# GQA decode step with a gated MLP: one w_out block in 16-row chunks over 4 row groups, the side table over 2, and half of wo folded

## The chip, the cores and the metric

The kernel runs on one core of one Trainium2 chip. The metric is the device time of one execution in microseconds (us); the figures below are the runs of the kernel before and one profiled execution of it. Engines are named as the profile names them: PE (TensorE matmuls), PEld (its weight loads), DVE (VectorE), ACT (ScalarE), POOL (GpSimd), SP (SyncE, which issues most of the loads). SPq and ACTq are the sequencers that issue DMAs. q1 is the DMA queue of SP's transfers, q10 that of ACT's; both are served by the same 16 DMA engines.

## The reference

One decode step with 8 batches, a width of 512, and everything in float32:

```python
xn = layernorm(x)                                   # x: (8, 1, 512)
q = (xn @ wq) -> (8, 32 heads, 1, 128)              # wq: (512, 4096)
k, v = caches (8, 8 kv heads, 4096, 128), each kv head for 4 query heads
p = softmax(q k^T / sqrt(128));  s = (p v) @ wo     # wo: (4096, 512)
z = gelu(xn @ w_in)                                 # w_in: (512, 1792)
z1 = z[:, :896];  z2 = layernorm(z[:, 896:])
g = w_sp * z2 + b_sp                                # w_sp, b_sp: one number each
gate = silu((z1 * g) @ w_out)                       # w_out: (896, 512)
out = x + s * gate
```

The two caches are 134 MB each, so nearly all of the 291 MB that the kernel reads is K and V.

## The kernel before

**Buffers.** Large loads go through a ring of three buffers of 128 partitions x 64 KB (`slot()`). They are used in this order: the MLP's weights (w_in and a part of w_out) in the first, `wq` in the second, the first half of K for head 0 in the third. The second half of K for head 0 takes the first buffer again, V's first half the second, and so on: for each of 8 heads two halves of K and two of V, 8 MB each, and at the end wo, also 8 MB, in seven pieces (`WO_PIECES`: 8, 8, 8, 4, 2, 1 and 1 of its 32 rows of heads). All of these are issued by SP in program order, and each waits until its buffer is free. Free means that every instruction that reads or writes the buffer has finished.

**Small loads.** ACT issues three: x (L52), the side table `side_sb` (L54), and `w_low` (L61). The side table has 128 rows of 130 numbers (520 bytes): x once more in the layout of the output, and in its last two columns w_sp and b_sp. `w_low` is the part of w_out that is not in the MLP's load: three of its seven blocks of 128 rows, cut into chunks of 32 rows. It lies in DRAM as 8 groups (`LOW_E`) of 4 rows, with 64 numbers of padding at the end of each group, and lands on 32 partitions of the first buffer. `from_slot` gives out what is left of the first buffer: to xn, to hT, and to e.

**The MLP** (`mlp()`) runs ahead of the projections. PE multiplies xn by w_in (L140), with four column groups of the array (32 columns each, output partitions 32 g to 32 g + 31) at work on four quarters of the columns. GELU and the layernorm of the second half follow on DVE, ACT and POOL. L171 applies w_sp and b_sp from the side table, L173 multiplies by z1. The product is transposed (L176 for the first 128 columns of each quarter into hT, L180 for the others in four chunks of 32 into hL), copied out of PSUM, and multiplied with w_out: L184 four blocks from the MLP's load, one in each column group; L188 the three blocks of w_low, four chunks for each. L190 to L200 bring the sum into the output's layout and form the gate.

**Behind it** PE runs `project_q` (L207, L213) for the two groups of four kv heads, then for each head the scores (L230), the softmax, and the values (L273, L282). `scr` is a pair of PSUM buffers which all short results take in turn.

**The end.** wo's rows of heads 0 to 27 (`FOLDED`) are multiplied at full width of 512 columns, with the four query heads of a kv head in the four column groups (L324). DVE copies this sum out (L327), and PE adds the four groups with the matrix `same` (L338). The last four rows of heads are multiplied in the output's layout directly, in four parts of 128 columns (L333), two ahead of the fold and two behind. DVE multiplies by the gate (L343), adds x from the side table (L344), and SP stores.

Of the kernel before, what the change touches and what calls it, by code (L numbers as in the profile page):

```python
# [13 lines left out]
P = 128  # L14
B, D = 8, 512
HKV, REP, S, DH = 8, 4, 4096, 128
NK = D // P
G = 4
J = S // (G * P)
R = 32  # L20
FH = 896
FQ = 256
NB = FH // P
# [3 lines left out]
UNIT = 2 * G * 512  # L27
SLOT = HALF * UNIT
WO_PIECES = [(0, 8), (8, 16), (16, 24), (24, 28), (28, 30), (30, 31), (31, 32)]
FOLDED = HKV * REP - REP  # L30
QR = P // 4
LOW_E = 8
N_LOW = (NB - G) * 4 * D


@with_exitstack
def tile_gqa_gmlp_decode(ctx: ExitStack, tc: tile.TileContext, x, side, kT, v, wq, wo,
                         w_mlp, w_low, out):
    nc = tc.nc
# [7 lines left out]
    def slot():  # L47
        return ring.tile([P, SLOT], F32, name="slot")
# [2 lines left out]
    x_sb = const.tile([B, D], F32, name="x_sb")  # L51
    nc.scalar.dma_start(x_sb, x)  # L52
    side_sb = const.tile([P, P + 2], F32, name="side_sb")
    nc.scalar.dma_start(side_sb, side)  # L54

    mlp_slot = slot()
    n_in, n_mlp = NK * 2 * FH, NK * 2 * FH + G * D
    n_low = n_mlp + N_LOW
    nc.sync.dma_start(mlp_slot[:, :n_mlp], w_mlp)
    w_in_sb = mlp_slot[:, :n_in].rearrange("p (k n) -> p k n", k=NK)  # L60
    nc.scalar.dma_start(mlp_slot[:QR, n_mlp:n_low],  # L61
                        w_low[:, :P // (4 * LOW_E) * N_LOW].rearrange("e (i n) -> e i n", n=N_LOW))
    w_out_sb = mlp_slot[:, n_in:n_mlp].rearrange("p (j d) -> p j d", j=G)
    w_low_sb = mlp_slot[:QR, n_mlp:n_low].rearrange("p (j a d) -> p j a d", a=4, d=D)
    spare = [n_low]

    def from_slot(rows, n):
        lo = spare[0]
        spare[0] = lo + n
        return mlp_slot[:rows, lo:lo + n]  # L70
# [6 lines left out]
    ident = const.tile([P, P], F32, name="ident")  # L77
# [26 lines left out]
    def scratch(shape, name):  # L104
        t = ps.tile([P, 512], F32, name="scr")
        n = 1
        for s in shape[1:]:
            n *= s
        return t[:shape[0], :n]
# [18 lines left out]
    def mlp():  # L128
        zu = work.tile([P, 4, FQ], F32, name="zu", tag="p")
        z, u = zu[:, :2], zu[:, 2:]  # L130
        hy = work.tile([P, 2 * D], F32, name="hy", tag="pT")
        y_sb, hL = hy[:, :D], hy[:QR, D:].rearrange("p (a s) -> p a s", a=4)
        pz = scratch([P, 2 * FQ], "pz")
        nc.vector.memset(pz, 0.0)
        for part in range(2):
            for k in range(NK):
                for g in range(G):
                    lo = g * FQ
                    n = min(FQ, FH - lo)
                    nc.tensor.matmul(pz[R * g:R * (g + 1), part * FQ:part * FQ + n], xnT[:, k, :],  # L140
                                     w_in_sb[:, k, part * FH + lo:part * FH + lo + n],
                                     start=(k == 0), stop=(k == NK - 1))
        zf, uf = z.rearrange("p a f -> p (a f)"), u.rearrange("p a f -> p (a f)")
        nc.vector.tensor_copy(zf, pz)
        nc.vector.tensor_mul(uf, zf, zf)
        nc.vector.tensor_scalar(uf, uf, 0.044715, 1.0, op0=ALU.mult, op1=ALU.add)
        nc.vector.tensor_mul(uf, uf, zf)
        nc.scalar.activation(uf, uf, AF.Tanh, scale=GELU_C)
        nc.vector.tensor_scalar(uf, uf, 1.0, 0.5, op0=ALU.add, op1=ALU.mult)
        nc.vector.tensor_mul(zf, uf, zf)  # L150

        def mean(src, name):
            part_sum = small.tile([P, 1], F32, name="part_sum")
            nc.vector.tensor_reduce(part_sum, src, op=ALU.add, axis=AX.X)
            pm = scratch([P, 1], "pm")
            nc.tensor.matmul(pm, same_all, part_sum, start=True, stop=True)
            t = small.tile([P, 1], F32, name=name)
            nc.vector.tensor_scalar(t, pm, 1.0 / FH, None, op0=ALU.mult)
            return t

        z1, z2 = z[:, 0, :], z[:, 1, :]
        mu = mean(z2, "mu")
        nc.vector.tensor_scalar(z2, z2, mu, None, op0=ALU.subtract)
        nc.vector.tensor_mul(u[:, 0, :], z2, z2)
        nc.vector.memset(u[(G - 1) * R:, 0, FH - (G - 1) * FQ:], 0.0)
        var = mean(u[:, 0, :], "var")
        nc.vector.tensor_scalar(var, var, EPS, None, op0=ALU.add)
        rs = small.tile([P, 1], F32, name="rs")
        nc.gpsimd.tensor_tensor(rs, var, neg_half, op=ALU.pow)
        nc.vector.tensor_scalar(z2, z2, rs, None, op0=ALU.mult)  # L170
        nc.vector.tensor_scalar(z2, z2, side_sb[:, P:P + 1], side_sb[:, P + 1:P + 2],  # L171
                                op0=ALU.mult, op1=ALU.add)
        nc.vector.tensor_mul(u[:, 1, :], z2, z1)  # L173
        hT = from_slot(P, P)
        th = scratch([P, P], "th")
        nc.tensor.transpose(th, u[:, 1, :P], ident)  # L176
        nc.vector.tensor_copy(hT, th)
        tl = scratch([QR, 4 * P], "tl")
        for a in range(4):
            nc.tensor.transpose(tl[:, a * P:(a + 1) * P], u[:, 1, P + a * QR:P + (a + 1) * QR], ident)  # L180
        nc.vector.tensor_copy(hL.rearrange("p a s -> p (a s)"), tl)
        pw = scratch([P, D], "pw")
        for g in range(G):
            nc.tensor.matmul(pw[R * g:R * (g + 1), :], hT[:, R * g:R * (g + 1)], w_out_sb[:, g, :],  # L184
                             start=True, stop=(g == G - 1))
        for a in range(4):
            for g in range(NB - G):
                nc.tensor.matmul(pw[R * g:R * (g + 1), :], hL[:, a, R * g:R * (g + 1)],  # L188
                                 w_low_sb[:, g, a, :], start=False, stop=(a == 3))
        nc.vector.tensor_copy(y_sb, pw)  # L190
        py = scratch([P, P], "py")
        for g in range(G):
            nc.tensor.matmul(py[R * g:R * (g + 1), :], same[:, 0, :], y_sb[:, g * P:(g + 1) * P],
                             start=True, stop=True)
        e = from_slot(P, P)
        nc.vector.tensor_scalar(e, py, -1.0, 87.0, op0=ALU.mult, op1=ALU.min)
        nc.scalar.activation(e, e, AF.Exp)
        nc.vector.tensor_scalar(e, e, 1.0, None, op0=ALU.add)
        nc.vector.reciprocal(e, e)
        nc.vector.tensor_mul(gate, py, e)  # L200
# [88 lines left out]
    def load_v(h, half, parts):  # L289
# [4 lines left out]
        return t.rearrange("p (i j e) -> p i j e", i=HALF, j=J)  # L294

    mlp()
    project_q(0)
    project_q(1)
# [22 lines left out]
    part, acc = sc[:, 0, :], sc[:, 1, :P]  # L321
    for m in range(FOLDED):
        h, r = divmod(m, REP)
        nc.tensor.matmul(part[R * r:R * r + B, :], oT[:, h, r, :], wo_sb[:, m, :],  # L324
                         start=(m < REP), stop=(m >= FOLDED - REP))
    part_sb = work.tile([P, D], F32, name="part_sb", tag="p")
    nc.vector.tensor_copy(part_sb, part)  # L327

    def last_head(lo, hi):
        for m in range(lo, hi):  # L330
            h, r = divmod(m, REP)
            for g in range(G):
                nc.tensor.matmul(acc[R * g:R * g + B, :], oT[:, h, r, :], wo_sb[:, m, g * P:(g + 1) * P],  # L333
                                 start=(m == FOLDED), stop=(m == HKV * REP - 1))

    last_head(FOLDED, FOLDED + 2)
    for g in range(G):
        nc.tensor.matmul(acc[R * g:R * g + B, :], same[:, 0, :B], part_sb[:, g * P:(g + 1) * P],  # L338
                         start=False, stop=False)
    last_head(FOLDED + 2, HKV * REP)  # L340

    res = const.tile([P, P], F32, name="res")
    nc.vector.tensor_mul(res, acc, gate)  # L343
# [42 lines left out]
```

## Time and profile before

| What | us |
|---|---|
| median of 3 runs | 685.25 (685.02 to 686.68) |
| the profiled execution | 687.51 |
| its span, first to last instruction | 685.7 |
| PE busy | 379.4 (55% of the span) |
| DVE busy | 173.8 (25%) |
| ACT busy | 13.5 (2%) |
| mean granted TensorE clock | 0.755 of full |

A time in the profile counts from the first instruction, so all positions in what follows are within the span of 685.7. The profiled execution itself is 1.8 us longer than its span and 2.3 us above the median.

How to read the lines: a line of a timeline begins with the start and the duration in us, then engine, source line, operation, and output<-inputs; `x24` is the number of instructions merged, and brackets hold the idle time ahead of it with what ended it. A float32 matmul is two instructions. In a list of waits the numbers are the total, the count and the longest. In a list of DMA queues they are packets, MB, and the time of those packets as a share of 16 engines over the stretch asked for; under it, a list of issues gives the size and the median time from the issue until the data is seen. A line of stretches gives its bounds, its length, the busy time of PE, PEld, DVE, ACT and POOL with the instructions, then the granted clock, the DMA share and GB/s.

### The profile page before, as it was taken

What the parts mean: (1) busy time and instruction counts of PE and PEld (TensorE: products, weight loads), DVE (VectorE), ACT (ScalarE), POOL (GpSimd) and SP (SyncE); (2) the same over time, 40 slices, a digit from 0 to 9 for tenths busy, and PEclk for the clock granted to TensorE, in tenths of its full rate; (3) what the DMA queues carried; (4) which work ended last, traced back from release to release, by engine and by line L of the source; (5) the groups of instructions that cost most, each with busy time, mean ns of one, the idle gap of its engine ahead of it and who ended that gap; (6) DMA issues with size and microseconds to landing.
All of it is one profiled execution on the core that took longest, in us unless ns stands there. A gap on an engine that the chain in (4) does not pass through costs nothing.

```text
span 685.7 us, 5701 instructions
## 1 busy us (share of the span) xinstructions
PE 379.4 (55%) x2557; PEld 113.3 (17%) x2557; DVE 173.8 (25%) x371; ACT 13.5 (2%) x27; POOL 3.7 (1%) x11
## 2 busy tenths in 40 slices
PE   1486464546665455455754464555655355555665
PEld 1121121112111111111211021111211021111221
DVE  2422042402430033401431024401421024401450
ACT  0000000000000000000000000000000000000000
POOL 1000000000000000000000000000000000000000
PEclk9768677767778777777787777767778777767787
DMA  9999999999999999999999999999999999999994
GB/s 402 421 448 422 428 429 432 444 432 440 425 429 432 433 440 440 429 433 428 429 432 429 424 440 433 443 433 432 433 432 426 428 429 440 441 432 438 399 427 182
DMA packets 6704, 291.23 MB, mean 425 GB/s; under 512 B 752, under 2 KB 1008, under 8 KB 1400
## 3 DMA queue, kind: packets, MB, share of 16 engines
q1 hardware_dynamic: 6480, 290.00, 98.1%
q10 hardware_dynamic: 200, 0.87, 0.3%
q8 instruction: 20, 0.33, 0.2%
q14 instruction: 4, 0.03, 0.0%
HBM read 290.80 MB, written 0.07 MB: 424 GB/s over the span
## 4 chain that ended last, share of the span: by engine, by line
DMA 81%; PE 17%; DVE 1%; issue 0%; ACTq 0%; SPq 0%
DMA slot<-in_kT 35%; DMA slot<-in_v 35%; PE sc L230 7%; PE o_ps L273 6%; DMA slot<-in_wo 6%; DMA slot<-in_w_low 5%; PE scr L207 1%; PE scr L188 1%; PE sc L324 1%; PE po_ps L282 0%; DVE o_sb L278 0%; DVE o_all L276 0%; PE sc L333 0%; SPq L310 0%; DVE q_sb L210 0%
## 5 line engine op out<-in xcount | busy, mean ns | idle before, releaser
L230 PE MATMUL sc<-slot,qz 128*32 128x512 f32 x1024 | 147.9, 742 | 135.9 <-DMA slot<-in_kT 135.9
L273 PE MATMUL o_ps<-slot,pT 128*16 128x512 f32 x1024 | 152.1, 734 | 75.0 <-DMA slot<-in_v 75.0
L276 DVE TENSOR_TENSOR o_all<-o_ps,diag 128x512 f32<-128x512 f32 x64 | 44.2, 691 | 149.6 <-PE o_ps L273 149.6
L235 DVE TENSOR_REDUCE nm<-sc 128x1 f32<-128x1024 f32 x8 | 9.8, 1224 | 280.5 <-PE sc L230 280.5
L230 PEld LDWEIGHTS sc<-slot,qz 128*32 128x32 f32 x1024 | 36.0, 133 | 241.4 <-DMA slot<-in_kT 140.1
L278 DVE TENSOR_REDUCE o_sb<-o_all 128x128 f32<-128x512 f32 x64 | 67.9, 1062 | 2.2
L273 PEld LDWEIGHTS o_ps<-slot,pT 128*16 128x16 f32 x1024 | 29.7, 111 | 155.4 <-issue 106.5
L282 PE MATMUL po_ps<-fold,o_sb 128*128 128x4 f32 x128 | 24.9, 264 | 28.0 <-DVE o_sb L278 28.0
L282 PEld LDWEIGHTS po_ps<-fold,o_sb 128*128 128x128 f32 x128 | 19.2, 189 | 72.9 <-DVE o_sb L278 72.9
L261 PE MATMUL scr<-ident,p 128*128 128x128 f32 x64 | 14.5, 404 | 10.7 <-DVE p L256 10.7
L237 ACT ACTIVATE p<-sc,nm 128x1024 f32<-128x1024 f32 x8 | 8.9, 1114 | 577.6 <-DVE nm L235 577.6
L263 DVE COPY pT<-scr 128x128 f32<-128x128 f32 x64 | 13.9, 283 | 9.2 <-PE scr L261 9.2
L261 PEld LDWEIGHTS scr<-ident,p 128*128 128x128 f32 x64 | 11.6, 207 | 11.1 <-issue 11.1
L324 PE MATMUL sc<-slot,oT 128*8 128x512 f32 x56 | 9.4, 800 | 3.2 <-DMA slot<-in_wo 3.2
L140 PE MATMUL scr<-slot,xnT 128*32 128x256 f32 (+1 forms) x64 | 5.6, 494 | 8.5 <-DMA slot<-in_w_mlp 8.5
L207 PE MATMUL scr<-slot,xnT 128*32 128x512 f32 x64 | 8.6, 686 | 0.0
L240 PE MATMUL scr<-ident,nm 128*1 128x128 f32 x8 | 2.2, 270 | 10.9 <-DVE nm L235 10.9
L188 PE MATMUL scr<-slot,hy 32*32 32x512 f32 x24 | 7.0, 1055 | 1.2 <-DMA slot<-in_w_low 1.2
L253 PE MATMUL scr<-wl,same 128*128 128x1 f32 x16 | 3.2, 271 | 6.2 <-DVE wl L251 6.2
L256 DVE TENSOR_SCALAR p<-p,w 128x1024 f32<-128x1024 f32 x8 | 6.0, 753 | 0.3
L219 DVE COPY qz<-scr 128x4 f32<-128x4 f32 x64 | 4.6, 148 | 1.5 <-PE scr L213 1.5
L140 PEld LDWEIGHTS scr<-slot,xnT 128*32 128x32 f32 x64 | 3.1, 148 | 10.6 <-issue 10.2
(86 smaller groups left out, 61.5 us busy)
## 6 DMA issues: line engine op xcount, KB each, us to landing
slot<-in_v SPq DMA_DIRECT2D x4, 2048.0 KB, 40.2
slot<-in_wo SPq DMA_DIRECT2D x3, 2048.0 KB, 41.6
slot<-in_w_mlp SPq DMA_DIRECT2D x1, 4608.0 KB, 13.7
slot<-in_wo SPq DMA_DIRECT2D x1, 1024.0 KB
slot<-in_w_low ACTq DMA_DIRECT2D x1, 768.0 KB
slot<-in_wo SPq DMA_DIRECT2D x1, 512.0 KB, 33.1
slot<-in_wo SPq DMA_DIRECT2D x2, 256.0 KB, 26.7
slot<-in_kT SPq DMA_DIRECT2D x16, 48.3
```

Source lines behind the costliest of these rows:

```text
L188: nc.tensor.matmul(pw[R * g:R * (g + 1), :], hL[:, a, R * g:R * (g + 1)], w_low_sb[:, g, a, :], start=False, stop=(a == 3))
L207: nc.tensor.matmul(pq[R * g:R * (g + 1), :], xnT[:, k, :], wq_sb[:, k, lo:lo + REP * DH], start=(k == 0), stop=(k == NK - 1))
L230: nc.tensor.matmul(sc[R * g:R * (g + 1), c, :], qz[:, h, b * R:(b + 1) * R], k_sb[:, i, c, g, :], start=(b == 0), stop=(b == B - 1))
L235: nc.vector.tensor_reduce(m, sc, op=ALU.max, axis=AX.XY, negate=True)
L237: nc.scalar.activation(p.rearrange("p j s -> p (j s)"), sc.rearrange("p c s -> p (c s)"), AF.Exp, bias=m, accum_out=l[:, h:h + 1])
L261: nc.tensor.transpose(t[:, j * P:(j + 1) * P], p[:, 4 * c + j, :], ident)
L263: nc.vector.tensor_copy(pT[:, 4 * c + j].rearrange("p b (g r) -> p g b r", g=G), t[:, j * P:(j + 1) * P].rearrange("p (g b r) -> p g b r", ...
L273: nc.tensor.matmul(of[R * c:R * c + G * REP, :], pT[:, j, b, :], v_unit[:, j], start=(j < G), stop=(j >= J - G))
L276: nc.vector.tensor_mul(o_all, o, diag[:, :, None].to_broadcast([P, G, DH]))
L278: nc.vector.tensor_reduce(o_sb, o_all.rearrange("p g d -> p d g"), op=ALU.add, axis=AX.X)
L282: nc.tensor.matmul(po[:, b * REP:(b + 1) * REP], o_sb, fold, start=True, stop=True)
L324: nc.tensor.matmul(part[R * r:R * r + B, :], oT[:, h, r, :], wo_sb[:, m, :], start=(m < REP), stop=(m >= FOLDED - REP))
```

## The change

Three things change.

- **w_out.** Six blocks (0, 2, 4, 6, 3, 5) come with the MLP's load, whose rows grow from 36,864 to 40,960 bytes. Block 1 alone is left in w_low, as 8 chunks (`CH`) of 16 rows, loaded as 4 groups of 4 rows on 16 partitions. hT now holds both halves of the transposed product, hL has 8 chunks, each copied by an instruction of its own. The main matmuls are 6 (block j in column group j // 2), the low ones 8, all of block 1, so in column group 0.
- **The side table** lies in DRAM as 2 padded groups of 64 rows and is loaded in that shape.
- **wo.** `FOLDED` is 16: rows of heads 0 to 15 are folded, 16 to 31 go direct, eight ahead of the fold and eight behind.

hT, y_sb and e move out of the first buffer's spare room into the work tiles hy and zu; hL moves into it.

```diff
-FOLDED = HKV * REP - REP
-QR = P // 4
-LOW_E = 8
-N_LOW = (NB - G) * 4 * D
+FOLDED = 16
+LOW_E, LOW_R = 4, 4
+QR = LOW_E * LOW_R
+CH = -(-P // QR)
+MAIN = [0, 2, 4, 6, 3, 5]
+LOW = [1]
+SIDE_E = 2
+SIDE_N = P // SIDE_E * (P + 2)
+N_LOW = len(LOW) * CH * D
...
-    nc.scalar.dma_start(side_sb, side)
+    nc.scalar.dma_start(side_sb, side[:, :SIDE_N].rearrange("e (p n) -> e p n", n=P + 2))
...
     nc.scalar.dma_start(mlp_slot[:QR, n_mlp:n_low],
-                        w_low[:, :P // (4 * LOW_E) * N_LOW].rearrange("e (i n) -> e i n", n=N_LOW))
+                        w_low[:, :LOW_R * N_LOW].rearrange("e (i n) -> e i n", n=N_LOW))
...
-        y_sb, hL = hy[:, :D], hy[:QR, D:].rearrange("p (a s) -> p a s", a=4)
+        hy2 = from_slot(P, CH * P).rearrange("p (a s) -> p a s", a=CH)
+        hT = hy[:, :2 * P].rearrange("p (a s) -> p a s", a=2)
+        hL = hy2[:QR]
+        y_sb, e = zu[:, :2].rearrange("p a f -> p (a f)"), zu[:, 2, :P]
...
-        hT = from_slot(P, P)
-        th = scratch([P, P], "th")
-        nc.tensor.transpose(th, u[:, 1, :P], ident)
-        nc.vector.tensor_copy(hT, th)
-        tl = scratch([QR, 4 * P], "tl")
-        for a in range(4):
-            nc.tensor.transpose(tl[:, a * P:(a + 1) * P], u[:, 1, P + a * QR:P + (a + 1) * QR], ident)
-        nc.vector.tensor_copy(hL.rearrange("p a s -> p (a s)"), tl)
+        th = scratch([P, 2 * P], "th")
+        for a in range(2):
+            nc.tensor.transpose(th[:, a * P:(a + 1) * P], u[:, 1, a * P:(a + 1) * P], ident)
+        nc.vector.tensor_copy(hT.rearrange("p a s -> p (a s)"), th)
+        for lo in range(0, CH, 4):
+            n = min(4, CH - lo)
+            tl = scratch([QR, n * P], "tl")
+            for a in range(lo, lo + n):
+                k = min(QR, P - a * QR)
+                nc.tensor.transpose(tl[:k, (a - lo) * P:(a - lo + 1) * P],
+                                    u[:, 1, P + a * QR:P + a * QR + k], ident)
+            for a in range(lo, lo + n):
+                k = min(QR, P - a * QR)
+                nc.vector.tensor_copy(hL[:k, a], tl[:k, (a - lo) * P:(a - lo + 1) * P])
         pw = scratch([P, D], "pw")
-        for g in range(G):
-            nc.tensor.matmul(pw[R * g:R * (g + 1), :], hT[:, R * g:R * (g + 1)], w_out_sb[:, g, :],
-                             start=True, stop=(g == G - 1))
-        for a in range(4):
-            for g in range(NB - G):
-                nc.tensor.matmul(pw[R * g:R * (g + 1), :], hL[:, a, R * g:R * (g + 1)],
-                                 w_low_sb[:, g, a, :], start=False, stop=(a == 3))
+        for i, j in enumerate(MAIN):
+            g, a = divmod(j, 2)
+            nc.tensor.matmul(pw[R * g:R * (g + 1), :], hT[:, a, R * g:R * (g + 1)], w_out_sb[:, i, :],
+                             start=(a == 0), stop=(j in (3, 5, 6)))
+        for a in range(CH):
+            k = min(QR, P - a * QR)
+            for i, j in enumerate(LOW):
+                g = j // 2
+                nc.tensor.matmul(pw[R * g:R * (g + 1), :], hL[:k, a, R * g:R * (g + 1)],
+                                 w_low_sb[:k, i, a, :], start=False, stop=(a == CH - 1))
...
-        e = from_slot(P, P)
...
-    last_head(FOLDED, FOLDED + 2)
+    late_wo(FOLDED, FOLDED + 8)
     for g in range(G):
         nc.tensor.matmul(acc[R * g:R * g + B, :], same[:, 0, :B], part_sb[:, g * P:(g + 1) * P],
                          start=False, stop=False)
-    last_head(FOLDED + 2, HKV * REP)
+    late_wo(FOLDED + 8, HKV * REP)
...
-        "side": side.reshape(P, P + 2),
+        "side": np.concatenate([side.reshape(SIDE_E, SIDE_N), np.zeros((SIDE_E, 64), np.float32)], axis=1),
```

`late_wo` is `last_head` under a new name, with the same body.

More of the change, by code (lines that the diff above doesn't have):

```diff
@@ L53, in tile_gqa_gmlp_decode @@
     side_sb = const.tile([P, P + 2], F32, name="side_sb")
-    nc.scalar.dma_start(side_sb, side)
+    nc.scalar.dma_start(side_sb, side[:, :SIDE_N].rearrange("e (p n) -> e p n", n=P + 2))
     mlp_slot = slot()
-    n_in, n_mlp = NK * 2 * FH, NK * 2 * FH + G * D
+    n_in, n_mlp = NK * 2 * FH, NK * 2 * FH + len(MAIN) * D
     n_low = n_mlp + N_LOW
@@ L61, in tile_gqa_gmlp_decode @@
     nc.scalar.dma_start(mlp_slot[:QR, n_mlp:n_low],
-                        w_low[:, :P // (4 * LOW_E) * N_LOW].rearrange("e (i n) -> e i n", n=N_LOW))
-    w_out_sb = mlp_slot[:, n_in:n_mlp].rearrange("p (j d) -> p j d", j=G)
-    w_low_sb = mlp_slot[:QR, n_mlp:n_low].rearrange("p (j a d) -> p j a d", a=4, d=D)
+                        w_low[:, :LOW_R * N_LOW].rearrange("e (i n) -> e i n", n=N_LOW))
+    w_out_sb = mlp_slot[:, n_in:n_mlp].rearrange("p (j d) -> p j d", d=D)
+    w_low_sb = mlp_slot[:QR, n_mlp:n_low].rearrange("p (j a d) -> p j a d", a=CH, d=D)
     spare = [n_low]
@@ L327, in tile_gqa_gmlp_decode, with late_wo @@
     nc.vector.tensor_copy(part_sb, part)
-    def last_head(lo, hi):
+    def late_wo(lo, hi):
         for m in range(lo, hi):
@@ L361 @@
     w2 = c(B_w_out).reshape(NB, P, D)
-    rows = P // (4 * LOW_E)
-    low = np.zeros((LOW_E, rows * N_LOW + 64), np.float32)
-    low[:, :rows * N_LOW] = w2[1::2].reshape(NB - G, 4, LOW_E, rows, D).transpose(2, 3, 0, 1, 4).reshape(LOW_E, -1)
+    low = np.zeros((len(LOW), CH * QR, D), np.float32)
+    low[:, :P] = w2[LOW]
+    low = low.reshape(len(LOW), CH, LOW_E, LOW_R, D).transpose(2, 3, 0, 1, 4).reshape(LOW_E, -1)
+    low = np.concatenate([low, np.zeros((LOW_E, 64), np.float32)], axis=1)
     arrays = {
         "x": x,
-        "side": side.reshape(P, P + 2),
+        "side": np.concatenate([side.reshape(SIDE_E, SIDE_N), np.zeros((SIDE_E, 64), np.float32)], axis=1),
         "kT": c(k.transpose(2, 0, 7, 1, 4, 6, 5, 3)).reshape(HKV, 2, P, SLOT),
@@ L373 @@
             c(B_w_in).reshape(NK, P, 2 * FH).transpose(1, 0, 2).reshape(P, NK * 2 * FH),
-            w2[0::2].transpose(1, 0, 2).reshape(P, G * D)], axis=1),
+            w2[MAIN].transpose(1, 0, 2).reshape(P, len(MAIN) * D)], axis=1),
         "w_low": low,
```

## The prediction

> **What bounds the kernel now.** I read the page's totals first, then the chain of waits, then what the SP queue waits for, and last the DMA queues in short windows of the first 60 us, where the change acts.
>
> ```profile
> span 685.7 us, 5701 instructions
> ...
> DMA  9999999999999999999999999999999999999994
> ...
> q1 hardware_dynamic: 6480, 290.00, 98.1%
> q10 hardware_dynamic: 200, 0.87, 0.3%
> ...
> DMA 81%; PE 17%; DVE 1%; issue 0%; ACTq 0%; SPq 0%
> ```
>
> The DMA engines are full in every slice but the last, and q1, the queue of SP's loads, alone fills 98.1% of them. So the end moves only by bytes added to the busiest DMA engine, by a stretch in which q1 runs dry, or by work behind the last load. The place where q1 can run dry lies at the start:
>
> ```profile
> SPq L286 <- DVE gate L200: 31.3, 1, 31.3
> ...
> 1.77 33.14 DMA slot<-in_w_low
> ...
> 45.87 0.33 SPq L286 DMA_DIRECT2D slot<-in_kT  x1
> ...
> 77.62 9.98 PE L230 MATMUL sc<-slot,qz 128*32 128x512 f32 x64 [9.88 <-DMA slot<-in_kT]
> ```
>
> Of the three buffers, the first holds the MLP's weights, the second wq, the third the first half of K. The second K half (issued at 45.87) has to wait until the MLP lets go of the first buffer, and SP stands in that wait for 31.3 us. What covers it is the queue behind the MLP weights:
>
> ```profile
> slot<-in_w_mlp SPq DMA_DIRECT2D x1, 4608.0 KB, 13.7
> slot<-in_w_low ACTq DMA_DIRECT2D x1, 768.0 KB
> side_sb<-in_side ACTq DMA_DIRECT2D x1, 65.0 KB, 17.8
> out<-res SPq DMA_DIRECT2D x1, 64.0 KB, 1.5
> ...
> q1 hardware_dynamic: 106, 6.42, 99.0%
> ```
>
> The last line is of the window 35 to 50 us: 6.42 MB / 16 engines / (0.99 x 15 us) = 27.0 GB/s for each DMA engine. The MLP weights land at 0.74 (their issue) + 13.7 = 14.4; wq and the first K half are 16.8 MB, 1.05 MB for each engine, 38.8 us. So q1 is dry at 53.3 us (as the consumer sees it) on engines that carry nothing else. The release at 45.87 comes some 7 us before: that is the whole cover.
>
> **The side table, the step that decides.** How does a queue share an engine with q1? Windows 1.6 to 5, 6.4 to 7.8 and 18.2 to 35 us:
>
> ```profile
> q1 hardware_dynamic: 32, 1.18, 98.6%
> q10 hardware_dynamic: 16, 0.02, 4.2%
> ...
> DMA packets 32, 0.60 MB, mean 427 GB/s; under 512 B 0, under 2 KB 16, under 8 KB 16
> ...
> q1 hardware_dynamic: 16, 0.59, 97.4%
> q10 hardware_dynamic: 16, 0.01, 2.0%
> ...
> DMA packets 160, 7.60 MB, mean 453 GB/s; under 512 B 24, under 2 KB 24, under 8 KB 24
> ...
> q10 hardware_dynamic: 48, 0.79, 10.9%
> ```
>
> In the second window 16 engines move 16 packets of q1 (36,864 bytes, a row of the MLP weights) and 16 of q10 (520 bytes, a row of the side table): one for one. A 520-byte row costs 2.0% of 16 x 1.4 us / 16 = 28 ns, but each waits a whole q1 packet for its turn. That is why 8 rows on an engine took 17.8 us to land. In the third window q10 moves 0.79 MB, the 32 rows of 24,576 bytes of w_low, and 16 packets under 512 bytes: 24 less the 8 of q1, which I read as each transfer's closing packet on each engine that it uses: 8 of the side table's 16 and 8 of w_low. So w_low, written as 8 padded groups, runs on 8 engines with 4 rows each.
>
> The side table gets the same form with 2 groups. I take it that it then runs on 2 engines with 64 rows each. In the first window each engine has had two q1 packets and no side row yet. An engine has 8 rows of the MLP weights, so a side row can go behind the second to the eighth of them (7), behind their closing packet (1), and behind the 8 rows and the closing packet of wq and of the K half (9 each): 26 turns. When q1 is dry, 64 - 26 = 38 rows are still to go. Alone on the engine they cost little:
>
> ```profile
> q1 hardware_dynamic: 144, 0.07, 36.7%
> ```
>
> This is the output store (window 684.1 to 684.7): 144 packets in 36.7% of 16 x 0.6 us, 24 ns each. Bounds for the 38 rows: nothing, and 38 x 0.19 = 7.2 us (1.5 us for the store's 8 rows on an engine). I take 0.9, since the store's packets are nearest in size.
>
> When does q1 dry now? Two more w_out blocks in w_mlp are 32,768 bytes more for each engine, 1.2 us; engines 0 and 1 also carry 18 more side rows by then (0.5 us). So 14.4 + 1.2 + 38.8 + 0.5 = 54.9, and the side table is seen at **55.9 us** instead of 19.2. L171 needs it:
>
> ```profile
> 29.69 0.41 DVE L171 TENSOR_SCALAR zu<-zu,side_sb 128x256 f32<-128x256 f32 x1
> 30.14 0.43 DVE L173 TENSOR_TENSOR zu<-zu 128x256 f32<-128x256 f32 x1
> ...
> 30.62 0.48 PE L176 MATMUL scr<-ident,zu 128*128 128x128 f32 x1 [2.38 <-DVE zu L173]
> ...
> 30.89 1.06 PE L180 MATMUL scr<-ident,zu 128*32 128x128 f32 x4
> 31.13 0.29 DVE L177 COPY slot<-scr 128x128 f32<-128x128 f32 x1 [0.57 <-PE scr L176]
> ...
> 31.88 1.94 PE L184 MATMUL scr<-slot 128*32 128x512 f32 x8
> ...
> 35.04 7.04 PE L188 MATMUL scr<-slot,hy 32*32 32x512 f32 x24 [1.23 <-DMA slot<-in_w_low]
> ```
>
> Behind L171 on DVE and PE stands everything: the MLP's tail, project_q, the first scores. On SP's queue the second K issue and with it every later load stand behind the release.
>
> **The chain from L171 to the release.** Up to the first transpose 0.9. Then 2 transposes for hT and 4 for hL before the first copies: L176 and L180 took 1.3 together for 5, so 1.6 for 6. Four copies of 16x128 instead of one 32x512: by L177's 0.29 (128x128) with gaps, 1.3; the scratch buffer that pw takes is theirs, so PE waits for them. The other 4 transposes and copies run beside that and the main matmuls. Main: L184's 8 instructions are four blocks side by side on the four column groups, 1.94; now 6 blocks, two rounds, 3.6. Low: L188's 24 instructions are 8 rounds of three side by side, 7.04 / 8 = 0.86 with the start left in it. Now all belong to block 1, that is to column group 0: 8 chunks x 2 instructions in single file, 16 x 0.855 = 13.7, with half the rows each but the same 512 columns. Bounds for one: 0.43 (full clock, below) and 0.86; I take the row. Sum: 0.9 + 1.6 + 1.3 + 0.1 + 3.6 + 13.7 = **21.2 us**. w_low's own 4 rows of 16,384 bytes follow the side table on engines 0 and 1, 65,536 / 27.0 = 2.4 us, and are there before the low matmuls begin. y_sb, hT and e now lie outside the buffer, so its release is the last low matmul, and no longer the gate: the 3.8 us from 42.08 to 45.87 fall away.
>
> Release: 55.9 + 21.2 + 0.1 = 77.2. From issue to sight, w_mlp took 13.7 for 10.9 us of bytes per engine (294,912 / 27.0): 2.8 of overhead. The second K half needs 19.4 + 2.8, and is seen at 99.4, against 77.6 before: **+21.8 us**, in which the DMA engines stand idle from about 54 to 78. That replaces, and isn't added to, the shifts of bytes among engines: 4 to 7 lose 64 KB, 8 to 15 gain 32 KB, 0 to 3 keep their sum, 0 and 1 gain 29 KB of side rows; all meet the restart empty.
>
> Is q1 fed after that? V's first half is issued after project_q, 11.3 us after the low matmuls (42.1 to 53.4 before): at 88.5, while K lands until 99. From then each buffer comes free as before, since landing and use keep their distance. None of the 21.8 is made up later, as the engines were full before.
>
> **The end.** wo's heads 16 to 27 go direct.
>
> ```profile
> 676.23 4.33 PE L324 MATMUL sc<-slot,oT 128*8 128x512 f32 x24 [3.00 <-DMA slot<-in_wo]
> ...
> 678.67 0.12 PEld L324 LDWEIGHTS sc<-slot,oT 128*8 128x8 f32 x8 [1.47 <-DMA slot<-in_wo]
> ...
> 680.63 0.69 DVE L327 COPY part_sb<-sc 128x512 f32<-128x512 f32 x1 [12.35 <-PE sc L324]
> 681.38 0.62 PE L333 MATMUL sc<-slot,oT 128*8 128x128 f32 x16 [0.81 <-DVE part_sb L327]
> ...
> 682.72 0.29 DVE L343 TENSOR_TENSOR res<-sc,gate 128x128 f32<-128x128 f32 x1 [1.40 <-PE sc L333]
> ```
>
> PE's work is the same: a folded head costs a quarter of a 512-column round, a direct one a 128-column round. But the copy (0.7) and the fold move ahead of the last loads. From 678.67 eight direct heads remain. At full clock they cost some 0.21 each (two heads in 0.62 with the start), at half 0.43: PE is through between 681.5, which the last piece's landing sets, and 682.3. Gain 0.4 to 1.2; I take 0.8. Nothing else gains.
>
> **Sum.** +21.8 - 0.8 = +21.0 on the profiled execution's 687.5 (span 685.7), so 708.5; on the median of the runs, 685.25, it gives **706**.
>
> **Rivals.**
>
> 1. The clock rises inside the low block. The rows:
>
> ```profile
> 14.50:18.70 4.20, 4.11 (x42) 2.39 (x45) 0.00 (x0) 0.00 (x0) 0.00 (x0) 1.00 0.86 372
> ...
> 35.00:42.10 7.10, 7.04 (x24) 1.49 (x24) 0.00 (x0) 0.00 (x0) 0.00 (x0) 0.50 1.02 443
> 42.80:46.00 3.20, 3.13 (x24) 1.13 (x28) 1.78 (x5) 0.31 (x1) 0.00 (x0) 0.50 0.99 430
> ```
>
> The granted clock (third number from the right) stayed at 0.50 through 7 us of unbroken low matmuls, so I take half. But now full-height matmuls run for 3.6 us right ahead. If they lift it, the low block costs 6.8 less: 699. [...]
>
> 2. Not slower: the side table is in early. The mechanism: q10 gets several rows per turn (or the table isn't confined to 2 engines), and it lands before L171 is ready at 29.7 + 1.2. It decides from some 6 rows per turn: 64 rows are then 11 turns, 8 of them by 15.6 us and 3 of 2.4 us, and w_low's 4 turns of 3.0 us and the closing packets bring it in at about 38, when the low matmuls are due. Release then 30.9 + 21.2 = 52.1, first bytes a little over 1 us later, 53.3, just as q1 dries. Engines 0 and 1 then end with 29 KB more than the busiest had, +1.1; with the tail's -0.8 that is 685.5. For it: only that no trace here shows so many rows on an engine; against it 16 to 16. [...]
>
> 3. The 38 rows drain slowly, at the store's 0.19: +6.3 more, 712.
>
> **How the numbers follow.** Forecast 62%, clock 20%, early side table 8%, slow drain 7%, 3% for something not thought of. The range, 697 to 712, takes in the first two with a part of the third bound. Within 0.3% (2 us, about what a measurement here tells from no change) lies rival 2 but for a little: same 5%, faster 4%, slower 91%.
>
> **What would show it.** Right: side_sb's landing near 54 us after its issue, L171 at about 56, DMA slices near 0 between 55 and 78 us, SP's second K issue near 77, the low matmuls 13.7 us at clock 0.50, the last 8 heads with no copy between them. Wrong: a side landing under 30 us, more than one side row per q1 packet, or full DMA slices up to 100 us.

## The result, and the profile after

The changed kernel took 706.38 us (median of 4 runs, 702.92 to 707.13) beside 685.13 for the kernel before (4 runs, 684.99 to 686.68): a ratio of 1.0295, 95% interval 1.0257 to 1.0333. Its profiled execution took 707.1 us, 19.6 more than that of before. The forecast was 706.

The page of the changed kernel, its totals, and the slices of its first 110 us:

```profile
span 705.3 us, 5853 instructions
...
DMA  9990799999999999999999999999999999999996
...
q1 hardware_dynamic: 6480, 290.52, 95.8%
...
DMA  8699998999999999889610000009888899989988
```

One hole is new, in the fourth slice of the page; in the finer row (2.75 us for each digit) the DMA engines are all but empty from about 55 to 74 us. q1's share of the engines falls from 98.1% to 95.8% for nearly the same bytes (290.0 and 290.5 MB). The timeline of the changed kernel around the hole, with the line numbers of the new file (L179 is L171 of before, L199 is L184, L205 is L188, L302 is L286, L246 is L230):

```profile
57.05 0.41 DVE L179 TENSOR_SCALAR zu<-zu,side_sb 128x256 f32<-128x256 f32 x1 [24.23 <-DMA side_sb<-in_side]
...
60.48 2.83 PE L199 MATMUL scr<-slot,hy 128*32 128x512 f32 x12
63.25 11.38 PE L205 MATMUL scr<-slot 16*32 16x512 f32 x16
74.66 0.33 SPq L302 DMA_DIRECT2D slot<-in_kT  x1
...
97.46 7.07 PE L246 MATMUL sc<-slot,qz 128*32 128x512 f32 x64 [2.69 <-DMA slot<-in_kT]
```

DVE stood 24.2 us for the side table, which came at 57.05 instead of 19.2. The low block ran 11.4 us in single file, SP could issue the second K half at 74.66 instead of 45.87, and PE had it at 97.46 instead of 77.62: 19.8 us later.

What SP waited for in the first 100 us of the changed kernel:

```profile
SPq L302 <- DMA slot<-in_w_low: 56.4, 1, 56.4
SPq L302 <- PE scr L205: 15.2, 1, 15.2
```

The first of these rows puts the wait down to w_low because its landing, at about 59 us, came last of those that the profile could tie to it. The release itself waited for L205; that w_low was no cause is seen from PE, which went from L199 to L205 without a gap.

Two windows show the turns. In the changed kernel from 20 to 50 us, and from 55 to 56.5 us (after q1 ran dry):

```profile
q1 hardware_dynamic: 204, 12.32, 98.8%
q10 hardware_dynamic: 25, 0.01, 0.1%
...
q10 hardware_dynamic: 83, 0.06, 12.0%
```

In 30 us q1 moved 204 packets on 16 engines, 12.8 on each. q10 moved 25, which is 12.5 on each of two engines: one for one. Then 83 went in 1.5 us. The packet records of that window have 80 rows of 520 bytes, 40 for each of two engines. The first two on each are the last turns, behind q1's last row and behind its closing packet; the other 38 follow 25 ns apart, as the prediction had counted them.

### The profile page after: what moved, and what is told of

Its sections match the earlier page's. It is cut to its first block, busy times and chain, and to the rows that moved or that the text cites. A ratio compares the mean times of both kernels' runs of the same rounds, so it can differ in the third digit from the quotient of the medians.

```text
span 705.3 us, 5853 instructions
## 1 busy us (share of the span) xinstructions
PE 381.4 (54%) x2630; PEld 118.5 (17%) x2630; DVE 174.9 (25%) x378; ACT 13.5 (2%) x27; POOL 3.7 (1%) x11
## 3 DMA queue, kind: packets, MB, share of 16 engines
q1 hardware_dynamic: 6480, 290.52, 95.8%
## 4 chain that ended last, share of the span: by engine, by line
DMA 73%; PE 17%; issue 4%; another core or an unknown queue 3%; DVE 1%; SPq 0%; POOLq 0%; POOL 0%; DVEq 0%
DMA slot<-in_kT 35%; DMA slot<-in_v 32%; PE sc L246 6%; DMA slot<-in_wo 6%; PE o_ps L289 6%; PE scr L205 2%; PE scr L223 1%; PE sc L349 1%; PE po_ps L298 0%; DVE o_sb L294 0%; PE scr L199 0%; DMA x_sb<-in_x 0%; DVE o_all L292 0%; DVE slot L195 0%
## 5 line engine op out<-in xcount | busy, mean ns | idle before, releaser
L246 PE MATMUL sc<-slot,qz 128*32 128x512 f32 x1024 | 143.3, 723 | 123.3 <-DMA slot<-in_kT 123.3
L246 PEld LDWEIGHTS sc<-slot,qz 128*32 128x32 f32 x1024 | 35.1, 130 | 225.0 <-DMA slot<-in_kT 131.1
L298 PEld LDWEIGHTS po_ps<-fold,o_sb 128*128 128x128 f32 x128 | 19.2, 189 | 73.4 <-DVE o_sb L294 73.4
L184 PE MATMUL scr<-ident,zu 128*128 128x128 f32 x2 | 0.7, 448 | 26.6 <-DVE zu L181 26.6
L205 PE MATMUL scr<-slot 16*32 16x512 f32 x16 | 11.4, 887 | 0.0
L349 PE MATMUL sc<-slot,oT 128*8 128x128 f32 x128 | 5.4, 337 | 3.1 <-DMA slot<-in_wo 3.1
L179 DVE TENSOR_SCALAR zu<-zu,side_sb 128x256 f32<-128x256 f32 x1 | 0.4, 413 | 24.2 <-DMA side_sb<-in_side 24.2
```

Source lines behind the costliest of these rows:

```text
L205: nc.tensor.matmul(pw[R * g:R * (g + 1), :], hL[:k, a, R * g:R * (g + 1)], w_low_sb[:k, i, a, :], start=False, stop=(a == CH - 1))
L246: nc.tensor.matmul(sc[R * g:R * (g + 1), c, :], qz[:, h, b * R:(b + 1) * R], k_sb[:, i, c, g, :], start=(b == 0), stop=(b == B - 1))
L298: nc.tensor.matmul(po[:, b * REP:(b + 1) * REP], o_sb, fold, start=True, stop=True)
```

## The experiments

Ten kernels, each timed in turns with the kernel before. That kernel's runs lay between 685.0 and 687.6 us, with a gap in the middle: about half near 685.2, half near 686.7. So its medians here (686.05 to 686.31) are above the 685.13 of the first comparison, and the ratios are what to compare.

| Kernel | Median us (runs) | Ratio to before | 95% interval |
|---|---|---|---|
| the change | 706.38 (4) | 1.0295 | 1.0257 to 1.0333 |
| e1: the change, side table as 128 rows | 684.70 (12) | 0.9978 | 0.9969 to 0.9987 |
| e2: before, side table in 2 groups | 701.89 (4) | 1.0222 | 1.0196 to 1.0247 |
| e3: before, 16 heads folded | 685.36 (12) | 0.9997 | 0.9988 to 1.0007 |
| e4: before, new cut of w_out alone | 684.72 (12) | 0.9983 | 0.9974 to 0.9992 |
| e5: before, side table in 4 groups | 698.76 (4) | 1.0198 | 1.0171 to 1.0225 |
| e6: before, side table in 8 groups | 696.26 (4) | 1.0152 | 1.0136 to 1.0168 |
| e7: the change, side table ahead on SP's queue | 685.74 (10) | 0.9998 | 0.9988 to 1.0007 |
| e8: the change, low chunks over four column groups | 697.56 (4) | 1.0170 | 1.0152 to 1.0187 |
| e9: no w_low, 128 side rows, 16 heads folded | 684.88 (11) | 0.9980 | 0.9971 to 0.9989 |
| e10: as e9, 28 heads folded | 685.13 (11) | 0.9990 | 0.9981 to 0.9998 |

### e1: take the side table's two groups back

```diff
-    nc.scalar.dma_start(side_sb, side[:, :SIDE_N].rearrange("e (p n) -> e p n", n=P + 2))
+    nc.scalar.dma_start(side_sb, side)
```

The table lies in DRAM in the matching shape, here and in e2.

> The changed kernel with the side table loaded as 128 rows again; everything else as changed. Theory (the late side table is the whole loss): the table is seen near 19 us again, L179 (its first use) runs at 30.9 us (29.7 before + 1.2 for the larger MLP load), the release of the first buffer follows 17.6 us later as in the changed kernel (21.2 at half clock throughout), 48.5 to 52.1, and the second K half's first bytes are there before q1 dries at about 54. Time 685.1 less the 0.8 of the new tail: 684.3 (683.3 to 685.5). Rival (the low block in single file costs by itself, side table or not): 690 or more, with empty DMA slices near 55 us.

The timeline of this kernel, and the DMA slices of its first 110 us:

```profile
30.80 0.41 DVE L179 TENSOR_SCALAR zu<-zu,side_sb 128x256 f32<-128x256 f32 x1
...
36.91 11.47 PE L205 MATMUL scr<-slot 16*32 16x512 f32 x16
48.40 0.33 SPq L302 DMA_DIRECT2D slot<-in_kT  x1
...
DMA  7699998999998899989898998999999889899998
```

The whole loss is gone: 684.70 us lies within the range expected, and the ratio of 0.9978 is even below 1. The low block is as slow as in the change (11.47), but now it ends at 48.4, while q1 still has work. The rival, a low block that costs by itself, falls.

### e2: the side table's two groups alone

```diff
-    nc.scalar.dma_start(side_sb, side)
+    nc.scalar.dma_start(side_sb, side[:, :SIDE_N].rearrange("e (p n) -> e p n", n=P + 2))
```

> The kernel before with the side table as 2 padded groups and nothing else. Theory: side_sb is seen near 55.9 us (57.05 in the changed kernel, less the 1.2 us of its larger MLP load), the release follows 16.2 us later (29.69 to 45.87 before) at 72.1, the second K half is seen 22.8 us after that (74.66 to 97.46 in the changed kernel) at 94.9 instead of 77.6: +17.3, so 702.4 (700 to 704). Rival (low block in single file is the loss): 685 to 690.

The timeline of this kernel and its slices of the first 110 us:

```profile
54.55 0.41 DVE L173 TENSOR_SCALAR zu<-zu,side_sb 128x256 f32<-128x256 f32 x1 [21.78 <-DMA side_sb<-in_side]
...
58.60 3.70 PE L190 MATMUL scr<-slot,hy 32*32 32x512 f32 x24
...
66.11 0.33 SPq L288 DMA_DIRECT2D slot<-in_kT  x1
...
DMA  7899998998899889988400009889999898989989
```

The median of 701.89 stands beside the 702.4 expected: this one edit makes the loss. The profiled execution was the fastest of the four, 698.22, with the low block (L190 here) at full clock, 3.70 instead of 7.04 us (587 ns for most of its matmul instructions; in the changed kernel's low block they took 587 at a granted 1.00 and 1,056 at 0.50); the others took 701.8 to 702.7. The difference of 3.3 us fits, but only the one run has a profile, so for the others the clock is argued. That the median came so near is in part luck. In the profile the release came at 66.11 instead of 72.1, and only 3.3 of these 6 us are the clock: the table came 1.35 us earlier than expected, and the wait of 1.23 us for w_low, which the 16.2 us of the expectation contain, fell away.

### e3: 16 heads folded, nothing else

```diff
-FOLDED = HKV * REP - REP
+FOLDED = 16
...
-    last_head(FOLDED, FOLDED + 2)
+    last_head(FOLDED, FOLDED + 8)
...
-    last_head(FOLDED + 2, HKV * REP)
+    last_head(FOLDED + 8, HKV * REP)
```

> The kernel before with wo's heads 16 to 31 direct, eight ahead of the fold and eight behind, and nothing else. Theory: the copy and the fold lie ahead of the last loads, 0.4 to 1.2 us less: 684.3 (683.9 to 684.9). Rival (the 48 more direct matmuls or their weight loads cost what the copy saves): 685.1 or more.

No difference that can be told: 0.9997 (0.9988 to 1.0007). The expected 684.3 was missed, and the time lies where the rival put it. The profiles show why the 0.8 us was too much. The ends of e3, e4 (28 heads folded) and e1 (16), two or three rows each:

```profile
675.03 3.32 PE L333 MATMUL sc<-slot,oT 128*8 128x128 f32 x64 [2.02 <-DMA slot<-in_wo]
...
680.66 0.29 DVE L343 TENSOR_TENSOR res<-sc,gate 128x128 f32<-128x128 f32 x1 [6.89 <-PE sc L333]
```
```profile
674.49 1.91 PE L340 MATMUL sc<-slot,oT 128*8 128x512 f32 x16 [1.32 <-DMA slot<-in_wo]
...
680.15 0.29 DVE L359 TENSOR_TENSOR res<-sc,gate 128x128 f32<-128x128 f32 x1 [1.40 <-PE sc L349]
```
```profile
674.48 1.93 PE L349 MATMUL sc<-slot,oT 128*8 128x128 f32 x64 [1.47 <-DMA slot<-in_wo]
...
679.40 0.41 PE L349 MATMUL sc<-slot,oT 128*8 128x128 f32 x8 [0.23 <-DMA slot<-in_wo]
679.87 0.29 DVE L359 TENSOR_TENSOR res<-sc,gate 128x128 f32<-128x128 f32 x1 [6.09 <-PE sc L349]
```

From the third piece of wo to the product with the gate: 5.63 us in e3 with PE partly at half clock (3.32 for 64 instructions that take 1.93 in e1); 5.66 in e4 at full clock with the old fold; 5.39 in e1 at full clock with the new, where the last piece's landing sets the end. So the new order saves 0.3 at full clock. It saved 0.9 beside the profile of before (6.49), whose fourth piece ran at half clock (granted 0.50 from 677.5 to 680.8 us). In e1, e3 and e4 the clock is read from the durations. One execution of each kernel was profiled, so how often the clock is at half there isn't known; both effects together are below what timing shows here. The rival's reason is not borne out: at full clock the third piece costs PE 1.93 us as direct heads (e1) and 1.91 folded (e4).

### e4: the new cut of w_out alone

The changed kernel with the side table as in e1 and the fold as before (`FOLDED = HKV * REP - REP`).

> The kernel before with w_out's new cut alone (six blocks in the MLP's load, one in 16-row chunks, hT, hL, y_sb and e where the change puts them); side table as 128 rows, 28 heads folded. Theory: the low block takes over 10 us in single file, but the release still comes by 52 us, under cover of q1: 685.1 (684.3 to 686.3). Rival (the single file costs its extra 4 to 7 us): 689 to 692.

The timeline of this kernel:

```profile
38.92 10.76 PE L205 MATMUL scr<-slot 16*32 16x512 f32 x16
...
49.71 0.33 SPq L302 DMA_DIRECT2D slot<-in_kT  x1
```

Measured 0.9983: the single file is wholly under cover, as its second K half was issued at 49.71. The new cut even gains 0.1 to 0.3%. Most of it is that the upper half of the times of before doesn't occur: none of the 12 runs is above 685.5, and beside the lower half (685.2) the gain is 0.5 us. e9 tries one reason and doesn't find it, so the cause stays open.

### e5 and e6: the side table in 4 and in 8 groups

In the kernel before, `SIDE_E` 4 and 8 in the form of the change; nothing else.

> The kernel before with the side table as 4 padded groups. Theory (a row waits for a turn, 26 turns until q1 dries): 32 rows on an engine, so 6 are left when q1 dries; the table is seen only about 0.7 us earlier than with 2 groups, and the time is within 1.5 us of that kernel: 701.5 (699.5 to 703.5). Rival (the delay goes with the number of rows on an engine): half of the loss with 2 groups, about 694.

> The kernel before with the side table as 8 padded groups: 16 rows on each of 8 engines, the same 8 that carry w_low. Theory: 8 rows go during the MLP load, 8 more at one per 2.4 us, the table is seen near 34 us and holds up L171 by 4 to 5 us; but w_low's 4 rows queue behind it and are seen near 49 instead of 35, so the low matmuls wait for them, the release comes near 60 and the second K half is seen near 82.7 instead of 77.6: +5, 690 (688 to 692). Rival (only the table's own delay counts): the release at 51 is under cover, 685.

The timelines of e5 and then of e6:

```profile
54.75 0.41 DVE L173 TENSOR_SCALAR zu<-zu,side_sb 128x256 f32<-128x256 f32 x1 [21.66 <-DMA side_sb<-in_side]
...
58.80 3.70 PE L190 MATMUL scr<-slot,hy 32*32 32x512 f32 x24
```
```profile
37.06 0.41 DVE L173 TENSOR_SCALAR zu<-zu,side_sb 128x256 f32<-128x256 f32 x1 [6.31 <-DMA side_sb<-in_side]
...
52.84 7.04 PE L190 MATMUL scr<-slot,hy 32*32 32x512 f32 x24 [11.75 <-DMA slot<-in_w_low]
...
63.31 0.29 DVE L202 TENSOR_TENSOR gate<-scr,slot 128x128 f32<-128x128 f32 x1
63.67 0.33 SPq L288 DMA_DIRECT2D slot<-in_kT  x1
...
86.88 9.62 PE L232 MATMUL sc<-slot,qz 128*32 128x512 f32 x64 [6.83 <-DMA slot<-in_kT]
```

With half the rows on an engine the table comes at the same time (54.75 against 54.55), because both have more rows than the 26 turns: the theory of turns holds, a delay by the number of rows would have brought it near 37 (19.2 and half of the 35.4 us that two groups add). The time was 2.7 us under the forecast of 701.5 and below its range; the profiled execution (698.64) had the low block at full clock (3.70 us, 587 ns as in e2).

With 16 rows the table fits into the turns, and the wait moves on to w_low, which queues behind it. That was forecast, but not its size: 696.3 instead of 690. The table came at 37.1 (forecast 34), w_low at 52.8 (49). By the packet records their last rows did start when forecast, at 34.0 and 48.9; but each transfer's closing packet waits for a turn of its own, 2.4 us here, and started only at up to 36.5 and 52.2. This further turn is most of the 3.1 and 3.8 us by which the two came later than forecast. It moved the release from near 60 to 63.67 and the second K half from 82.7 to 86.88. That is 4.2 of the missed 6.3 us; the rest isn't traced. In the kernel before, the gate's input e lies in the first buffer, so the release comes 3.8 us after the low block. That is the edit of the change that did its part: in the changed kernel SP issued right at the end of the low block.

### e7: the same two groups, but on SP's queue ahead of the MLP's weights

```diff
+    nc.sync.dma_start(side_sb, side[:, :SIDE_N].rearrange("e (p n) -> e p n", n=P + 2))
     nc.sync.dma_start(mlp_slot[:, :n_mlp], w_mlp)
```

The line on ACT's queue is gone; the rest is the changed kernel.

> The changed kernel, side table still in 2 groups, but issued by SP ahead of the MLP weights, so that it shares q1 with them and waits for no turns. Theory: side_sb is seen by 5 us, the 64 rows cost engines 0 and 1 some 1.6 us, L179 runs at 33 to 35, the release comes at 51 to 55, little or no dry stretch: 685.5 (684 to 688). Rival (two engines for 128 short rows are the cost, whatever the queue): 700 or more.

The timeline of this kernel, and its slices of the first 110 us:

```profile
34.76 0.41 DVE L179 TENSOR_SCALAR zu<-zu,side_sb 128x256 f32<-128x256 f32 x1
...
52.37 0.33 SPq L302 DMA_DIRECT2D slot<-in_kT  x1
...
DMA  5799899889999989999998988999998989999999
```

685.74, a ratio of 0.9998. The same 64 rows on each of two engines cost 1 us beside e1 and not 21, where they wait for no turns. So the loss is neither the two engines nor the short rows, but the queue beside q1.

### e8: shorten the chain behind the late table

```diff
+                c = a % G
-                nc.tensor.matmul(pw[R * g:R * (g + 1), :], hL[:k, a, R * g:R * (g + 1)],
-                                 w_low_sb[:k, i, a, :], start=False, stop=(a == CH - 1))
+                nc.tensor.matmul(pw[R * c:R * (c + 1), :], hL[:k, a, R * g:R * (g + 1)],
+                                 w_low_sb[:k, i, a, :], start=False, stop=(a >= CH - G))
```

The main matmuls no longer end a sum (`stop=False`), as each column group now ends with a low chunk.

> The changed kernel with the eight low chunks spread over the four column groups (their partial sums are added by the same matrix afterwards, the result is unchanged), so that four run side by side. Theory: the low block takes 1.8 to 3.4 us instead of 11.4, the release comes 8.0 to 9.6 us earlier behind the same late side table, and the dry stretch is that much shorter: 697.6 (696 to 699). Rival (the end doesn't hang on this chain): 706.

The timeline of this kernel:

```profile
56.58 0.41 DVE L179 TENSOR_SCALAR zu<-zu,side_sb 128x256 f32<-128x256 f32 x1 [23.28 <-DMA side_sb<-in_side]
...
60.01 3.64 PE L199 MATMUL scr<-slot,hy 128*32 128x512 f32 x12
63.58 1.96 PE L206 MATMUL scr<-slot 16*32 16x512 f32 x16
65.69 0.33 SPq L303 DMA_DIRECT2D slot<-in_kT  x1
```

1.96 instead of 11.38 us, and 697.56 us, the 697.6 forecast. The release came 9.0 us earlier than in the changed kernel (65.69 and 74.66), the end 8.8. Behind a late table every microsecond of the chain is a microsecond of the end; in e1, with the table early, the same 11.4 us cost nothing.

### e9 and e10: no w_low at all

All seven blocks in the MLP's load, no low block, side table as 128 rows:

```diff
-MAIN = [0, 2, 4, 6, 3, 5]
-LOW = [1]
+MAIN = [0, 2, 4, 6, 1, 3, 5]
...
```

The code and the load of w_low go with it.

> No w_low at all: all seven w_out blocks come with the MLP's load (seven main matmuls in two rounds of column groups, no low block), the side table is loaded as 128 rows, wo folded for 16 heads. Theory (beside the side table, what a kernel of this form loses or gains is the bytes on its busiest DMA engine): in the kernel before, 8 engines carry 96 KB more than the others, with the new cut 4 engines carry 64 KB more and the rest 32 KB; without w_low all carry 48 KB more than the lightest of before, 48 KB less than its busiest, 1.8 us at 27.0 GB/s: 683 (682 to 684.5). The stretch between the first and the last engine's end of a load shrinks to what the instruction fetches leave, under 3 us. Rival (the gain of the kernel with 16 heads folded and 128 side rows came from the release or the tail, not from balance): 684.7.

> As the kernel without w_low, but with 28 heads folded, as before. Theory: the direct heads gain only where PE is at half clock at the end; at full clock the last landing sets the end for both. 0.2 to 0.9 us more than with 16 heads: 683.5 (682.5 to 685). Rival (the direct heads gain nothing): the same time within 0.1%.

The theory of the busiest engine fell, at least in its size: 684.88, outside its range, no better than e1 and where the rival put it. From the packet records, the end of three loads on the last engine, and by how much it is behind the first:

```
            V, head 0, 1st    V, head 4, 1st    V, head 7, 1st
            last    spread     last    spread    last    spread
before      96.4    5.5        407.6   7.1       639.7   6.9
e1          95.8    3.7        406.4   4.6       639.0   4.9
e9          94.6    1.9        405.8   3.5       639.4   4.9
```

At first e9 is 1.8 us ahead of the kernel before, just what the bytes would give. By the last head less than 0.3 is left, as the spread has grown from 1.9 to 4.9, partly in two steps of 1.1 and 1.2 us (between the loads that end at 307.8 and 328.3, and at 580.2 and 600.7). Something delays single engines on the way by as much as the lead. The instruction fetches are a candidate (the page of e9):

```profile
q8 instruction: 20, 0.33, 0.2%
```

20 packets in 0.2% of 16 x 683 us are 1.1 us each. One of them lies in each of the two stretches with a step (at 312.2 and 589.5), but others lie in stretches without one. Which engines they fall on isn't in the profile, so this stays argued. e10 (685.13, just outside its range) is 0.25 us above e9, and the intervals of their ratios overlap; this fits the theory (0.2 to 0.9) as well as its rival (the same within 0.1%), so it decides nothing.

## Why the prediction was right, point by point

**The side table's turns.** Forecast 55.9 us, measured 57.05. The count of rows left when q1 ran dry (38) was exact, and they drained at 25 ns (24 taken). Of the 1.1 us, 0.6 came from q1, whose last row on the later of the two engines ended at 55.5 us by the packet records (54.9 forecast); the rest lies between the table's last packet, at 56.5, and L179. e7 and the pair e2 and e5 show that it is the turns, and not the engines or the rows.

**One small term was missed.** With the side rows confined to two engines, w_low's four rows now take their turns during the MLP load on the engines that carry w_low but no side rows: by the packet records eight rows of 16,384 bytes, 0.61 us each, between 7.2 and 14.4 us. The issue rows of the changed kernel:

```profile
slot<-in_w_mlp SPq DMA_DIRECT2D x1, 5120.0 KB, 17.0
```

13.7 + 1.2 would be 14.9 (e1 has 15.5). It cost nothing here, as L179 waited for the table anyway.

**The chain to the release.** Forecast 21.2 us, measured 17.6 (57.05 to 74.66). The low block was sized at 13.7 and took 11.4, the main block at 3.6 and took 2.8, and the steps ahead of it at 3.9 and took 3.4. The windows of the changed kernel show the reason in the granted clock, third number from the right:

```profile
58.00:62.00 4.00, 3.89 (x18) 1.69 (x20) 2.15 (x9) 0.00 (x0) 0.00 (x0) 0.50 0.03 12
62.00:65.40 3.40, 3.40 (x13) 0.74 (x8) 0.00 (x0) 0.00 (x0) 0.00 (x0) 0.94 0.00 0
65.40:66.90 1.50, 1.50 (x4) 0.43 (x3) 0.00 (x0) 0.00 (x0) 0.00 (x0) 0.63 0.00 0
66.90:74.70 7.80, 7.72 (x10) 1.23 (x8) 0.04 (x1) 0.00 (x0) 0.00 (x0) 0.50 0.00 0
```

So the first rival came in by a third: the clock rose during the main block, and it fell back in the middle of the low block. e1, e4 and e7 show the same, with the clock at full from 35.9 to 39.4, 38.7 to 42.1 and 40.8 to 44.2 us and at half for the rest of the low block. That such a rise comes could have been read from the kernel before. Its first MLP matmuls of 256 columns (L140) took 0.63 us each until 18.4 us and 0.38 from 18.8 on, some 4 us into that block. The 1.00 in the prediction's row of 14.5 to 18.7 misleads: the trace holds no clock record ahead of 18.7, and the durations show half clock: these matmuls start 0.43 us apart in a column group until 18.4, and 0.21 from 18.8 on, where the record has 1.00. In the changed kernel the records have the rise at 62.4 us, 1.9 us into the main block, and the fall at 65.8, 3.4 us later, where PE was busy without a gap. What sets the one or the other isn't shown.

**From release to landing.** Forecast 22.2 us, measured 22.8. With 1.1 late and 3.6 early the second K half was 19.8 us late instead of 21.8.

**Afterwards.** No second hole opened, as forecast, and nothing was made up. At the third piece of wo the lag was 20.4 us (676.23 to 696.67), 0.6 more than at the second K half. The end of the changed kernel:

```profile
696.67 3.09 PE L349 MATMUL sc<-slot,oT 128*8 128x128 f32 x64 [3.09 <-DMA slot<-in_wo]
...
699.93 2.30 PE L349 MATMUL sc<-slot,oT 128*8 128x128 f32 x64
702.29 0.29 DVE L359 TENSOR_TENSOR res<-sc,gate 128x128 f32<-128x128 f32 x1 [7.96 <-PE sc L349]
```

5.62 us to the product with the gate, 6.49 before: 0.9 of gain in this pair of profiles, 0.8 forecast. e3 shows that it is no steady gain: by itself it can't be told in the time.

**The sum.** +19.6 us in the profiled pair (20.4 less 0.9, rounded), +21.0 forecast. The median came nearer still, but partly by luck: the chain was 3.6 too long, the table 1.1 too early, the profiled execution of before lies 2.3 us above its median and that of the change only 0.7, and the runs of the changed kernel spread over 4 us.

**The second rival**, several rows per turn, is out: the rows on ACT's queue (25 on two engines beside 204 packets of q1 on 16) went one at a time.

**The edits are not additive.** Alone, the cut of w_out gains 0.17% and the fold nothing that shows; the table's form loses 2.2%. Together they lose 2.95%, because the late table puts the slow low block onto the path. The change without that one edit (e1) beats both kernels: 684.7 us, 0.22% under the kernel before.

## What to carry to other kernels

Count the rows that a small transfer puts on one DMA engine, not its bytes. In these runs each row beside q1 waited for one of its packets (25 rows on two engines beside 204 packets on 16 in the changed kernel, 2.4 us for 64 KB), the closing packet waited once more (2.4 us in e6), and w_low, queued behind the table, came at 52.8 us in e6 instead of 34.9. So put a small table that is needed early ahead of the bulk loads on their own queue (e7: 685.74 us, a ratio of 0.9998), or spread it over all engines (e1: 684.70, 0.9978). And an edit that is free under cover should be priced again when another edit takes the cover away.

## What was not expected

The TensorE clock fell from full to half in the middle of unbroken work: PE was busy for all but 0.1 us from 62 to 74.7, yet the clock went from 0.94 over 62 to 65.4 to 0.50 from 66.9 on. The matmuls of the low block use 16 rows and 32 columns of the array, and whether that is the reason was not tested; in e8, where four of them run side by side, the whole block was over in 1.96 us and shows no fall (587 to 664 ns for each matmul instruction). Less expected, too, was that a lead of 1.8 us from evenly spread bytes (e9) shrinks to less than 0.3 over the run while the engines drift apart by 3 us.
